# Idle row tiles of score waves filled with zero matmuls, and the last four output projections accumulated early, in a two-branch attention kernel

## The chip, the cores and the metric

The kernel runs on one core of one Trainium2 chip. The metric is the device time of the whole program in microseconds (us). Engines: PE multiplies matrices (TensorE), ACT is the scalar engine, DVE the vector engine, POOL is GpSimd, SP issues most DMAs. "Throttled window" means a stretch in which the profile shows PE's granted clock at 0.5; they are counted in units of 3.41 us, the length of a single one in the traces (three in a row: 10.24 us in that of the kernel before).

## The reference, cut to what matters

```python
S, D, H, Dh = 2048, 512, 32, 16
# branch A: softmax attention          # branch B: linear attention
scores = einsum("bhqd,bhkd->bhqk", q, k) * Dh**-0.5
a = (softmax(scores) @ v) @ wo_A
b = (phi(q) (phi(k)^T v) / (phi(q) . sum phi(k))) @ wo_B
out = g * a + (1 - g) * b              # g = sigmoid(x . gate_w), one number per row
```

Branch A needs 32 heads x 2048 x 2048 = 134 million exponentials, which fixes the shape of the kernel.

## The kernel before

The kernel is laid out at build time by a scheduler of its own, written into the kernel file. It keeps an estimated clock for each engine and at every step emits the candidate that fits best.

The work is cut into 32 rounds. A round is four heads (those of one parity among eight) for 512 queries: four row tiles of PE (32 rows each) hold the four heads. A *score unit* is one matmul with 32 rows of K as weights and 512 queries moving; units run side by side in one wave if they use different row tiles (a wave of four took 0.40 us in the trace of the kernel before, at 93.66 us, and the mean record of one matmul is 0.387). ACT takes the units in groups of three and two banks; DVE takes blocks of four units and computes the exponential with integer operations.

```python
gsets = [(0, 1, 2), (3, 4)]            # banks of ACT's groups: 3 units, 2 units, 3, 2, ...

def emit_act_group(c):
    ...
    for k, (r, kb, j) in enumerate(units):          # j: row tile of the unit
        l, q, _ = kq_aps(r, kb, j)
        fns.append(mm(BK[set_[k]], l, q))
    ride = d_ride(set(u[2] for u in units)) if n >= 2 else None   # DVE's units may ride in the same wave
    ...
    pe(fns, reads=rd, writes=wr2, waves=1, m="row", cols=128 * len(fns))
    op(AC, lambda: nc.scalar.activation(PT[...], ps[...], ACT.Exp, scale=SCALE), ...)

def warm_mm(gap):                      # "warm waves": fill PE's idle time, meant to keep its clock up
    if apos[0] >= NR or warm_count() >= WARMC:      # columns x tiles of the last 3.413 us
        return False
    ...                                # four column tiles, 17 columns of zeros each, into the accumulator
```

A wave with three units, or with two and no rider, leaves one or two row tiles idle. The accumulator `acc` is one bank into which the products of probabilities and V go, one round after the other.

Output projections: an output block of 128 rows is the sum of eight matmuls, four with branch B's numbers (transposed by DMA into `OBT`) and four with branch A's (`OT`); the last of these needs the end of the last round.

```python
def t_num(qc, q):                      # branch B: numerator, then four DMA transposes of the block
    ...
    for i in range(4):
        raw = dma(OBT[:, s, i, ...], OB[:, sl, ...], f"obt{sl}", reads=[r_OB[sl]],
                  writes=[r_OBT[s][q]] + (r_phiK[0:8] if i == 0 else []), transpose=True, lat=2.5 + i)

def t_out(qc, q):                      # eight matmuls into one bank, a copy, a DMA out
    ...
    if qc == NQC - 1 and q % 2:        # the last four: odd ones copied by ACT, even ones by DVE
        op(AC, lambda: nc.scalar.copy(outt[:, sl, :], BK[b]), reads=[r_bk[b]],
           writes=[r_outt[sl], r_wA[2], r_wv1], cost=0.48)
    ...

# main loop
if apos[0] >= NR - 1 and dst["cur"] is None and progress() > TAILP:
    maxhold[0] = 2                     # how many banks such tasks may hold at once
if apos[0] >= NR:                      # all exponentials emitted
    maxhold[0] = 6
    MISCB[:] = [6, 5] + list(range(5))
```

At the start, DVE sets to 1.0 the seventeenth column of each head of V (which gives the sums of the softmax): 512 elements of each of 128 partitions, 34 bytes apart.

The profile names a buffer by the memory that it shares: `OBT` appears there as sb_phiK, and `OB` and the rows of the output as sb_wA.

The softmax here doesn't subtract the row's maximum and nothing guards it: scores larger than these inputs give would overflow.

Of the kernel before, what the change touches and what calls it, by code (L numbers as in the profile page):

```python
# [18 lines left out]
SEMLAT = 0.05  # L19
# [126 lines left out]
def bass_gated_mix__mha_block__linear_attn_block__prompt_kernel(  # L146
# [12 lines left out]
    Dh = D // H  # L159
# [5 lines left out]
    NR = NQC * 8  # L165
# [7 lines left out]
    with ExitStack() as es:  # L173
# [164 lines left out]
        def mcost(m, waves):  # L338
            return (0.0 if m == mode[0] else 0.095) + 0.015 + 0.2145 * waves

        def pe(fns, reads=(), writes=(), waves=1.0, m="full", cols=None):
            deps = _deps_for(PE, reads, writes)
            n = len(fns)
            first = None
            cost = mcost(m, waves)
            mode[0] = m
            for k, fn in enumerate(fns):
                ev = PE.add(fn, deps if k == 0 else (), inc=(k == n - 1), cost=cost / n, lag=0.155)
                if k == 0:
                    first = ev  # L350
            first.t = ev.t
            c = 512.0 * waves if cols is None else cols
            hist.append((PE.clock, c))
            COLS.append((PE.clock, c))
            hsum[0] += c
            for res in reads:
                res.r[PE] = first
            for res in writes:
                res.w = ev
                res.r = {}  # L360
            return ev

        def mm(o, l, r, start=True, stop=True, sg=False):
# [11 lines left out]
        def load_xT(t, cc, lat):  # L375
# [29 lines left out]
        op(PO, lambda: nc.gpsimd.affine_select(out=identb[:], in_=identb[:], compare_op=ALU.not_equal,  # L405
                                               fill=1.0, base=0, pattern=[[-1, 128]], channel_multiplier=1),
           reads=[r_ident], writes=[r_ident])
        op(PO, lambda: nc.gpsimd.memset(ones[:], 1.0), writes=[r_const])
        op(PO, lambda: nc.gpsimd.memset(Zsel[:], 0.0), writes=[r_Zsel])
        op(PO, lambda: nc.gpsimd.tensor_copy(pidx[:], pidx_i[:]), reads=[r_pidx], writes=[r_mask])  # L410
# [218 lines left out]
        def t_num(qc, q):  # L629
            s = qc % 2  # L630
            sl = q % 4
            b = yield "bank"
            rd = r_phiQT[s] + [r_KVbd]
            yield ("pe", rd, [r_bk[b]], 1.4)
            pe([mm(BK[b][:, 128 * i:128 * (i + 1)], phiQT[:, s, i, 128 * q:128 * (q + 1)], KVbd[:, i, :]) for i in range(4)],
               reads=rd, writes=[r_bk[b]], waves=1.4, cols=512)
            yield ("dve", [r_bk[b], r_denB], [r_OB[sl]])
            op(DV, lambda: nc.vector.tensor_tensor(OB[:, sl, :].rearrange("p (h d) -> p h d", h=32), BK[b].rearrange("p (h d) -> p h d", h=32),
                                                   denB[:, q, :].unsqueeze(2).to_broadcast([128, 32, 16]), ALU.mult),
               reads=[r_bk[b], r_denB], writes=[r_OB[sl], r_wA[1]], cost=0.69)  # L640
            yield "free"
            for i in range(4):
                raw = dma(OBT[:, s, i, 128 * q:128 * (q + 1)], OB[:, sl, 128 * i:128 * (i + 1)], f"obt{sl}",
                          reads=[r_OB[sl]], writes=[r_OBT[s][q]] + (r_phiK[0:8] if i == 0 else []), transpose=True, lat=2.5 + i)

        def t_out(qc, q):
            s = qc % 2
# [37 lines left out]
        MPRI = 1.5  # L685
        DHUNG = -1
        DFAR = 0.8
        TAILP = 31.5
        D0 = .8
        DR0 = 1  # L690
        WARMC = 6000
# [56 lines left out]
        def need(key):  # L748
            t = bykey.get(key)
            if t is not None and not t.done:  # L750
                STATS.setdefault("forced", []).append((key, round(PE.clock, 1)))
                finish(t)

        def progress():
            return cur_units[0] / 64.0

        def misc_candidates():
            now = PE.clock
            p = progress()
            n = 0  # L760
            for t in list(tasks):
                if not t.started:
                    if t.nb > p or any(not bykey[k].done for k in t.pre):
                        continue
                if t.req == "bank":
                    free = [b for b in MISCB if b not in held]
                    if not free or len(held) >= maxhold[0]:
                        continue
                    yield (max(now, bank_free(min(free, key=bank_free)) + SEMLAT), "bank", t, 1.0)
                    n += 1  # L770
                    if n >= 3:
                        break
                    continue
                if t.done:
                    continue
                if t.req[0] == "wait":
                    if bykey[t.req[1]].done:
                        yield (now, "wait", t, 0.0)
                    continue
                if t.req[0] == "dve":  # L780
                    rt = _ready(DV, t.req[1], t.req[2]) + SEMLAT
                    if rt <= max(DV.clock, now) + 0.02:
                        yield (now, "dve", t, 0.0)
                    else:
                        yield (rt - 0.02, "dve", t, 0.0)
                else:
                    yield (_ready(PE, t.req[1], t.req[2]) + SEMLAT, "pe", t, t.req[3])
                n += 1
                if n >= 3:
                    break  # L790


# [46 lines left out]
        def act_group_cand():  # L839
# [16 lines left out]
            ready = max(_ready(PE, rd, wr), pt_free - 0.3) + SEMLAT  # L856
            return ready, units, set_, rd, wr, slot

        def emit_act_group(c):
            ready, units, set_, rd, wr, slot = c  # L860
            n = len(units)
            fns = []
            for k, (r, kb, j) in enumerate(units):
                l, q, _ = kq_aps(r, kb, j)
                fns.append(mm(BK[set_[k]], l, q))
            ride = d_ride(set(u[2] for u in units)) if n >= 2 else None
            rd, wr2 = list(rd), list(wr)
            if ride is not None:
                banks, js, rrd = ride
                fns += d_mms(banks, js)  # L870
                rd += [x for x in rrd if x not in rd]
                wr2 += [r_bk[b] for b in banks]
            pe(fns, reads=rd, writes=wr2, waves=1, m="row", cols=128 * len(fns))
            op(AC, lambda: nc.scalar.activation(PT[:, slot, 0:512 * n], ps[:, 512 * set_[0]:512 * (set_[0] + n)], ACT.Exp,  # L874
                                                scale=SCALE),
               reads=wr, writes=[r_PT[slot]], cost=EXC[n])
            if ride is not None:
                d_s1(banks, js)
            last = units[-1]
            for r in range(units[0][0], last[0]):  # L880
                act_done[r] = True
            for k, (r, kb, j) in enumerate(units):
                front[r] = max(front[r], kb + 1)
                pv_left[r] += 1
                pvq.append((r, kb, j, slot, k))
            ptleft[slot] = n
            apos[0], apos[1] = last[0], 4 * last[1] + last[2] + 1
            cur_units[0] = 64 * last[0] + 4 * last[1] + last[2] + 1
            while apos[0] < NR and apos[1] >= 4 * (NTB - claimed[apos[0]]):
                act_done[apos[0]] = True  # L890
                apos[0], apos[1] = apos[0] + 1, 0
            gcount[0] += 1
# [94 lines left out]
        dst = {"cur": None, "n": 0}  # L987
        chainq = collections.deque()
        lastd = [False]
        RES = .2  # L990
        CHG = .2
        CHI = 0.1
# [130 lines left out]

        def emit_d(c):
            _, banks, js, rd = c
            pe(d_mms(banks, js), reads=rd, writes=[r_bk[b] for b in banks], waves=1, m="row", cols=128 * len(js))
            d_s1(banks, js)

        def chain_op(_=None):
# [108 lines left out]
        need(("K", 0, 0))  # L1238
        need(("Q", 0, 0))
        op(DV, lambda: nc.vector.memset(QP[:, 1:3], 0.0), writes=r_QP[1] + r_QP[2], cost=0.9)  # L1240
        op(DV, lambda: nc.vector.memset(V[:].rearrange("p t h c -> p (t h) c")[:, :, Dh:Dh + 1], 1.0), writes=[x for v in r_V for x in v], cost=0.6)
        guard = 0
        while True:
            guard += 1
# [1 line left out]
            now = PE.clock  # L1246
            if progress() > MH2:
                maxhold[0] = 1
            if apos[0] >= NR - 1 and dst["cur"] is None and progress() > TAILP:
                maxhold[0] = 2  # L1250
            if apos[0] >= NR:
                maxhold[0] = 6
                MISCB[:] = [6, 5] + list(range(5))
            ca = act_group_cand()
# [26 lines left out]
            if not cands:  # L1281
                if not tasks and apos[0] >= NR and not pvq and not dpv:
                    break
                if apos[0] >= NR:
                    for t in tasks:
                        t.nb = -1
                    continue
                raise AssertionError(("stuck", apos, acc_round, len(pvq), [t.key for t in tasks][:5]))
            pmode = {0: "row", 0.7: "row", MPRI: "full", 1: "row", 2: "col", 3: "col", 4: "full"}
            avail = sorted((c for c in cands if c[0] <= now + 0.02),  # L1290
                           key=lambda c: (c[1] > 0 and c[2] > 0, c[1] if c[1] <= 0.7 else 1 if pmode[c[1]] == mode[0] else 2, c[1]))
            pick = None
            for c in avail:
                if c[1] == 0 or c[2] == 0.0 or now + c[2] <= must:
# [75 lines left out]
```

## Time and profile before

| | before |
|---|---|
| time, median of 3 runs | 792.84 us (791.65 to 794.0) |
| span in the profile | 790.4 us |
| ACT / PE / DVE busy | 96% / 94% / 89% |
| first exponential | 9.76 us |
| last exponential ends | 778.4 us |
| throttled windows of 3.41 us | 6 |

The page of the kernel before, its head: span, busy us and share of each engine, then the granted clock of PE in 40 equal slices (9 is 0.9 or more).

```profile
span 790.4 us, 17903 instructions
PE 743.7 (94%) x7815; PEld 227.3 (29%) x7877; DVE 701.7 (89%) x1009; ACT 760.6 (96%) x692; POOL 7.6 (1%) x35
...
PEclk9999889999999999999999999999999999999999
...
ACT 73%; PE 16%; DVE 7%; issue 3%; DMA 1%; SPq 0%
```

The last line is the chain of waits that ended last: it runs 73% through ACT. PE and DVE are nearly as full, but much of PE's time is warm waves that nobody waits for. So the first question of any change here is what it does to ACT: its work, and the time in which it waits.

The table of stages of the kernel before: stretch, its length, then busy us and count for PE, PE's weight loads, DVE, ACT and POOL, then the granted clock, the DMA share and GB/s.

```profile
0.00:20.00 20.00, 15.07 (x126) 6.83 (x127) 8.45 (x18) 10.27 (x10) 6.43 (x31) 1.00 0.80 187
80.00:100.00 20.00, 17.02 (x178) 6.70 (x174) 16.84 (x42) 17.24 (x16) 0.00 (x0) 0.86 0.00 1
100.00:120.00 20.00, 19.52 (x155) 4.94 (x157) 16.92 (x26) 17.59 (x17) 0.00 (x0) 0.89 0.03 7
420.00:440.00 20.00, 18.54 (x215) 5.17 (x208) 17.18 (x23) 18.70 (x18) 0.00 (x0) 0.91 0.18 57
440.00:460.00 20.00, 18.45 (x193) 5.16 (x195) 18.80 (x29) 19.09 (x19) 0.00 (x0) 0.91 0.01 2
760.00:780.00 20.00, 19.52 (x232) 5.62 (x230) 17.96 (x22) 17.67 (x17) 0.00 (x0) 0.92 0.01 2
```

ACT is busy for 20.00 of 20 us in most stretches. The largest exceptions are shown: the start, and stretches in which the clock is below 1. There ACT waits for scores while PE runs at half clock for a part of the stretch. In the last stretch only 0.63 us are such a wait; the rest of the missing 2.3 us is the end, since the last exponential is done at 778.4.

Three places of the trace of the kernel before, in order of time: start, length, engine, line, operation, output and inputs, count, and in brackets the idle time before and what ended it. First the ones of V on DVE, and the second wait of ACT at the start:

```profile
12.70 0.48 DVE L1241 MEMSET sb_V<- 128x512 bf16 x1 [1.70 <-issue]
14.52 1.02 ACT L874 ACTIVATE sb_PT<-ps 128x1024 bf16<-128x1024 f32 x1 [1.05 <-PE ps L364]
```

Then the gate: sixteen small copies on DVE, then the eviction that frees a bank, then the scores that waited for the bank, then ACT. The clock falls to 0.5 just after this, for three windows (94.23 to 104.47 us).

```profile
89.55 3.24 DVE L534 COPY sb_gT<-sb_g 32x16 f32<-32x16 f32 x16
92.82 0.69 DVE L1115 TENSOR_SCALAR sb_Lb<-ps 128x512 uint16<-128x512 f32 x1
93.66 0.40 PE L364 MATMUL ps<-sb_QP,sb_KT 32*128 32x512 bf16 x4 [1.89 <-DVE sb_Lb L1115]
94.10 2.36 ACT L874 ACTIVATE sb_PT<-ps 128x1536 bf16<-128x1536 f32 x2 [1.64 <-PE ps L364]
```

Last the end: the final transpose of branch A's output, then 25 matmuls (the list shows the first and the last group), and the last copy.

```profile
781.21 0.71 DVE L983 STREAM_TRANSPOSE sb_OT<-sb_Tn 128x512 bf16<-128x512 bf16 x1
781.98 0.39 PE L364 MATMUL ps<-sb_phiK,sb_OT 128*128 128x512 bf16 x1 [1.30 <-DVE sb_OT L983]
...
786.52 1.03 PE L364 MATMUL ps<-sb_phiK,sb_OT 128*128 128x512 bf16 x4
787.59 0.59 ACT L664 CAST sb_wA<-ps 128x512 bf16<-128x512 f32 x1 [2.87 <-PE ps L364]
```

### The profile page before, as it was taken

The numbers are of one execution on the slowest core, as the hardware profiler recorded it, in microseconds if no ns is written. First come the engines' busy times: TensorE is split into PE (matmuls) and PEld (weight loads), VectorE is DVE, ScalarE is ACT, GpSimd is POOL, SyncE is SP. The second block draws the span as 40 slices with busy tenths as digits, with TensorE's granted clock in tenths as the row PEclk, the third lists the DMA queues.
The fourth block names the chain that finished last, engine by engine and source line by source line (L and its number), as shares of the span: only waits on it lengthen the run. The fifth ranks groups of instructions, "written<-read, shape, count | busy, mean of one in ns | idle before, by whom it ended". The sixth has DMA issues, their size and how long they took to land.

```text
span 790.4 us, 17903 instructions
## 1 busy us (share of the span) xinstructions
PE 743.7 (94%) x7815; PEld 227.3 (29%) x7877; DVE 701.7 (89%) x1009; ACT 760.6 (96%) x692; POOL 7.6 (1%) x35
## 2 busy tenths in 40 slices
PE   7999899999999999999999999999999999999997
PEld 3333322222222222332222223223222332232222
DVE  4398889899999999989998999988999898899995
ACT  5999889999999999999999999999999999999994
POOL 3000000000000000000000000000000000000000
PEclk9999889999999999999999999999999999999999
DMA  7200000000000000102002000010001001000000
GB/s 185 70 7 2 1 7 2 7 2 9 2 5 4 2 7 2 36 1 61 2 2 61 1 8 9 16 33 8 14 17 31 10 13 24 27 10 17 12 2 27
DMA packets 31342, 14.93 MB, mean 19 GB/s; under 512 B 19104, under 2 KB 31264, under 8 KB 31264
## 3 DMA queue, kind: packets, MB, share of 16 engines
q1 hardware_dynamic: 29392, 13.00, 6.3%
q8 instruction: 62, 1.02, 0.5%
q10 hardware_dynamic: 1872, 0.79, 0.4%
q14 instruction: 16, 0.13, 0.1%
HBM read 6.55 MB, written 2.10 MB: 11 GB/s over the span
## 4 chain that ended last, share of the span: by engine, by line
ACT 73%; PE 16%; DVE 7%; issue 3%; DMA 1%; SPq 0%
ACT sb_PT L874 71%; PE ps L364 16%; DVE sb_Lb L1115 2%; ACT sb_ebuf L542 2%; DVE sb_Xb L1142 1%; DVE sb_Xb L1136 1%; DMA sb_xT<-in_A_x_dram 1%; DVE sb_Eb L1139 0%; DVE sb_Lb L1145 0%; DVE sb_gT L534 0%; DVE sb_Tn L979 0%; DVE sb_OT L983 0%; DVE sb_U L964 0%; DVE sb_QP L482 0%; DVE sb_phiK L546 0%
## 5 line engine op out<-in xcount | busy, mean ns | idle before, releaser
L874 ACT ACTIVATE sb_PT<-ps 128x1536 bf16<-128x1536 f32 (+1 forms) x655 | 752.3, 1420 | 16.6 <-PE ps L364 16.0
L364 PE MATMUL ps<-sb_QP,sb_KT 32*128 32x512 bf16 x2048 | 312.1, 387 | 25.9 <-ACT sb_PT L874 13.3
L1115 DVE TENSOR_SCALAR sb_Lb<-ps 128x512 uint16<-128x512 f32 (+1 forms) x302 | 264.8, 878 | 47.8 <-PE ps L364 46.0
L364 PEld LDWEIGHTS ps<-sb_QP,sb_KT 32*128 32x128 bf16 x2048 | 77.5, 91 | 283.8 <-ACT sb_PT L874 213.8
L364 PE MATMUL ps<-sb_PT,sb_V 128*17 128x512 bf16 x1636 | 155.7, 388 | 1.8 <-DVE sb_U L964 1.4
L364 PE MATMUL ps<-sb_warm 128*17 128x512 bf16 (+8 forms) x2074 | 147.0, 341 | 1.6 <-POOL sb_warm L402 1.3
L1142 DVE TENSOR_TENSOR sb_Xb<-sb_Xb,sb_Lb 128x2048 bf16<-128x2048 bf16 x103 | 125.1, 1214 | 0.0
L1136 DVE TENSOR_SCALAR sb_Xb<-sb_Lb 128x2048 uint16<-128x2048 uint16 x103 | 70.7, 686 | 1.4
L1139 DVE TENSOR_SCALAR sb_Eb<-sb_Lb 128x2048 uint16<-128x2048 uint16 x103 | 70.3, 683 | 0.0
L1145 DVE TENSOR_SCALAR sb_Lb<-sb_Lb 128x2048 uint16<-128x2048 uint16 x103 | 70.2, 682 | 0.0
L364 PEld LDWEIGHTS ps<-sb_PT,sb_V 128*17 128x17 bf16 x1636 | 37.2, 87 | 99.0 <-issue 89.4
L364 PEld LDWEIGHTS ps<-sb_warm 128*17 128x17 bf16 (+1 forms) x2077 | 48.2, 91 | 51.6 <-issue 27.0
L364 PE MATMUL ps<-sb_Eb,sb_V 128*17 128x512 bf16 x412 | 40.9, 388 | 0.2 <-DVE sb_Eb L1139 0.2
L364 PE MATMUL ps<-sb_Xb,sb_V 128*17 128x512 bf16 x412 | 40.4, 383 | 0.3 <-DVE sb_Xb L1142 0.2
L364 PE MATMUL ps<-sb_Lb,sb_V 128*17 128x512 bf16 x412 | 40.4, 382 | 0.1
L364 PE MATMUL ps<-sb_xT,sb_wA 128*128 128x512 bf16 x89 | 28.2, 395 | 3.1 <-issue 2.4
L964 DVE STREAM_TRANSPOSE sb_U<-ps 128x512 f32<-128x512 f32 x32 | 22.6, 708 | 3.6 <-PE ps L364 3.6
L542 ACT ACTIVATE sb_ebuf<-ps 128x512 bf16<-128x512 f32 x32 | 25.3, 791 | 0.0
L364 PE MATMUL ps<-sb_wA,sb_xT 128*128 128x128 bf16 (+1 forms) x128 | 19.0, 275 | 0.2
L364 PE MATMUL ps<-sb_xT,sb_wBx 128*128 128x512 bf16 x56 | 17.4, 383 | 1.5 <-issue 1.0
L364 PE MATMUL ps<-sb_phiK,sb_OT 128*128 128x512 bf16 x62 | 17.5, 382 | 1.3 <-DVE sb_OT L983 1.3
L466 DVE CAST sb_KT<-ps 128x512 bf16<-128x512 f32 x16 | 11.0, 685 | 8.0 <-PE ps L364 8.0
(80 smaller groups left out, 300.1 us busy)
## 6 DMA issues: line engine op xcount, KB each, us to landing
sb_QP<-sb_QT SPq DMA_DIRECT2D x120, 16.0 KB, 1.8
out_dram<-sb_wA SPq DMA_DIRECT2D x14, 128.0 KB, 1.8
sb_wA<-in_A_wqkv_dram SPq DMA_DIRECT2D x2, 512.0 KB, 6.5
sb_wBx<-in_B_wqkv_dram SPq DMA_DIRECT2D x2, 512.0 KB, 6.2
sb_xnat<-in_A_x_dram SPq DMA_DIRECT2D x2, 512.0 KB, 4.0
sb_phiK<-sb_wA SPq DMA_TRANSPOSE x64, 2.3
sb_xnat<-in_A_x_dram SPq DMA_DIRECT2D x3, 256.0 KB, 3.2
sb_wBv<-in_B_wqkv_dram SPq DMA_DIRECT2D x1, 512.0 KB, 8.5
```

Source lines behind the costliest of these rows:

```text
L364: return lambda: nc.tensor.matmul(o, lhsT=l, rhs=r, start=start, stop=stop, skip_group_check=sg)
L466: op(DV, lambda: nc.vector.tensor_copy(KT[:, t8, 512 * t:512 * (t + 1)], BK[b]), reads=[r_bk[b]], writes=[r_KT[t8][t]], cost=0.69)
L542: op(AC, lambda: nc.scalar.activation(ebuf[:, s, :], BK[b], ACT.Exp), reads=[r_bk[b]], writes=[r_e[s]], cost=0.48)
L874: op(AC, lambda: nc.scalar.activation(PT[:, slot, 0:512 * n], ps[:, 512 * set_[0]:512 * (set_[0] + n)], ACT.Exp, scale=SCALE), reads=wr, w ...
L964: op(DV, lambda: nc.vector.transpose(U[:, par, :], acc), reads=[r_acc], writes=[r_U[par]], cost=0.71)
L1115: op(DV, lambda: nc.vector.tensor_scalar(Lb[:, sl, 512 * k:512 * (k + n)], src, S1A, S1B, op0=ALU.mult, op1=ALU.add), reads=[r_bk[b] for b ...
L1136: op(DV, lambda: nc.vector.tensor_scalar(X, L, 0x7F, 0x3F00, op0=ALU.bitwise_and, op1=ALU.bitwise_or), reads=[rl], writes=[rx], cost=CH[0])
L1139: ev = op(DV, lambda: nc.vector.tensor_scalar(E_, L, 0xFF80, None, op0=ALU.bitwise_and), reads=[rl], writes=[re_], cost=CH[1])
L1142: ev = op(DV, lambda: nc.vector.tensor_tensor(xb, xb, lb, ALU.mult), reads=[rx, rl], writes=[rx], cost=CH[2])
L1145: ev = op(DV, lambda: nc.vector.tensor_scalar(L, L, float(EXP_SH), None, op0=ALU.add), reads=[rl], writes=[rl], cost=CH[3])
```

## The change

Its intent is threefold. A wave with an idle row tile gets one more matmul, a *filler*: 32 rows x 128 columns of zeros as weights, 512 columns moving, added to the accumulator, so that PE's clock falls less often. All four last output projections hold a bank each and do what they can before the last round ends. And two smaller things: the ones of V are set by POOL, and the four transposes of a block no longer wait for one another.

```diff
+        def fill(fns, rd, wr, used):
+            free = [j for j in range(4) if j not in used]
+            lj, lev = lastf
+            if lj in free:
+                free = [lj]
+            elif lev is not None and lev.t + 0.3 > PE.clock:
+                free = []
+            if FILL and free and apos[0] < NR and warm_count() < FILLC and _ready(PE, (), [r_acc]) + SEMLAT <= PE.clock:
+                j = free[0]
+                ...                    # another row tile than last time: wait for the last filler
+                fns.append(mm(acc, warm[32 * j:32 * j + 32, 0:128], warm[32 * j:32 * j + 32, :], start=False, stop=False, sg=True))
+                rd.append(r_warm)
+                wr.append(r_acc)
@@ emit_act_group, and the same in emit_d
+            fill(fns, rd, wr2, [u[2] for u in units] + (ride[1] if ride is not None else []))
+        FILL = 1
+        FILLC = 5200
@@ start
+        op(PO, lambda: nc.gpsimd.memset(V[...][:, :, Dh:Dh + 1], 1.0), ...)
-        op(DV, lambda: nc.vector.memset(V[...][:, :, Dh:Dh + 1], 1.0), ...)
@@ t_num
-                          reads=[r_OB[sl]], writes=[r_OBT[s][q]] + (r_phiK[0:8] if i == 0 else []), ...)
+                          reads=[r_OB[sl]], writes=[r_OBT[s][q]] + r_phiK[0:8] if i == 0 else [], ...)
+            r_OBT[s][q].w = _Raw(...)  # the block is there when the last of the four is
@@ main loop
-            if apos[0] >= NR - 1 and dst["cur"] is None and progress() > TAILP:
+            if apos[0] == NR - 1 and dst["cur"] is None and d_claim() is None:
+                lastp[0] = 32.0        # lets the last four projections start
                 maxhold[0] = 2
             if apos[0] >= NR:
+                lastp[0] = 32.0
                 maxhold[0] = 6
@@ choice among what is ready, once all exponentials are out: full-array work comes last
-   ... 1 if pmode[c[1]] == mode[0] else 2 ...
+   ... 5 if ended and pmode[c[1]] == "full" else 1 if pmode[c[1]] == mode[0] else 2 ...
```

(Cut: four instead of three tasks are looked at after the end, and bookkeeping of the waits.)

More of the change, by code (lines that the diff above doesn't have):

```diff
@@ L339, in mcost @@
             return (0.0 if m == mode[0] else 0.095) + 0.015 + 0.2145 * waves
+        fdeps = []
+        filler = [False]
         def pe(fns, reads=(), writes=(), waves=1.0, m="full", cols=None):
-            deps = _deps_for(PE, reads, writes)
+            deps = _deps_for(PE, reads, writes) + fdeps
+            fdeps.clear()
             n = len(fns)
@@ L360, in pe @@
                 res.r = {}
+            if filler[0]:
+                filler[0] = False
+                lastf[1] = ev
             return ev
@@ L407, in bass_gated_mix__mha_block__linear_attn_block__prompt_kernel @@
            reads=[r_ident], writes=[r_ident])
+        op(PO, lambda: nc.gpsimd.memset(V[:].rearrange("p t h c -> p (t h) c")[:, :, Dh:Dh + 1], 1.0), writes=[x for v in r_V for x in v], cost=0.6)
         op(PO, lambda: nc.gpsimd.memset(ones[:], 1.0), writes=[r_const])
@@ L643, in t_num @@
                 raw = dma(OBT[:, s, i, 128 * q:128 * (q + 1)], OB[:, sl, 128 * i:128 * (i + 1)], f"obt{sl}",
-                          reads=[r_OB[sl]], writes=[r_OBT[s][q]] + (r_phiK[0:8] if i == 0 else []), transpose=True, lat=2.5 + i)
+                          reads=[r_OB[sl]], writes=[r_OBT[s][q]] + r_phiK[0:8] if i == 0 else [], transpose=True, lat=2.5 + i)
+            r_OBT[s][q].w = _Raw(dma_sems[f"obt{sl}"][0], dma_sems[f"obt{sl}"][1], raw.t)
+            r_OBT[s][q].r = {}
+            for x in r_phiK[0:8]:
+                x.w = r_OBT[s][q].w
         def t_out(qc, q):
@@ L687, in bass_gated_mix__mha_block__linear_attn_block__prompt_kernel @@
         DFAR = 0.8
-        TAILP = 31.5
         D0 = .8
@@ L752, in need @@
                 finish(t)
+        lastp = [0.0]
         def progress():
-            return cur_units[0] / 64.0
+            return max(lastp[0], cur_units[0] / 64.0)
         def misc_candidates():
@@ L770, in misc_candidates @@
                     n += 1
-                    if n >= 3:
+                    if n >= (4 if apos[0] >= NR else 3):
                         break
@@ L788, in misc_candidates @@
                 n += 1
-                if n >= 3:
+                if n >= (4 if apos[0] >= NR else 3):
                     break
@@ L857, in act_group_cand @@
             return ready, units, set_, rd, wr, slot
+        lastf = [None, None]
+        def fill(fns, rd, wr, used):
[7 more added lines that the diff above has]
+                j = free[0]
+                lastf[0] = j
+                filler[0] = True
+                if j != lj and lev is not None:
+                    fdeps.append(_Raw(PE.sem, PE.cover(lev.idx), lev.t))
+                fns.append(mm(acc, warm[32 * j:32 * j + 32, 0:128], warm[32 * j:32 * j + 32, :], start=False, stop=False, sg=True))
+                rd.append(r_warm)
+                wr.append(r_acc)
         def emit_act_group(c):
@@ L1125, in emit_d @@
             _, banks, js, rd = c
-            pe(d_mms(banks, js), reads=rd, writes=[r_bk[b] for b in banks], waves=1, m="row", cols=128 * len(js))
+            fns, rd, wr = d_mms(banks, js), list(rd), [r_bk[b] for b in banks]
+            fill(fns, rd, wr, js)
+            pe(fns, reads=rd, writes=wr, waves=1, m="row", cols=128 * len(fns))
             d_s1(banks, js)
@@ L1240, in bass_gated_mix__mha_block__linear_attn_block__prompt_kernel @@
         op(DV, lambda: nc.vector.memset(QP[:, 1:3], 0.0), writes=r_QP[1] + r_QP[2], cost=0.9)
-        op(DV, lambda: nc.vector.memset(V[:].rearrange("p t h c -> p (t h) c")[:, :, Dh:Dh + 1], 1.0), writes=[x for v in r_V for x in v], cost=0.6)
         guard = 0
@@ L1288, in bass_gated_mix__mha_block__linear_attn_block__prompt_kernel @@
                 raise AssertionError(("stuck", apos, acc_round, len(pvq), [t.key for t in tasks][:5]))
+            ended = apos[0] >= NR
             pmode = {0: "row", 0.7: "row", MPRI: "full", 1: "row", 2: "col", 3: "col", 4: "full"}
             avail = sorted((c for c in cands if c[0] <= now + 0.02),
-                           key=lambda c: (c[1] > 0 and c[2] > 0, c[1] if c[1] <= 0.7 else 1 if pmode[c[1]] == mode[0] else 2, c[1]))
+                           key=lambda c: (c[1] > 0 and c[2] > 0, c[1] if c[1] <= 0.7 else 5 if ended and pmode[c[1]] == "full" else 1 if pmode[c[1]] == mode[0] else 2, c[1]))
             pick = None
```

## The prediction

> **What bounds it now.** ScalarE. The page gives ACT 96% busy, PE 94%, DVE 89% of 790.4 us. The chain of waits is 71% exponentials. The stage table in 20 us slices shows ACT at 20.00 of 20 almost everywhere, so only ACT's 29.8 us of idleness and its own work can be saved: about 9.8 before the first exponential at 9.76 us and some 1.5 soon after; 5.2 in 80 to 120; 2.2 in 420 to 460; 2.3 in 760 to 780, of which 0.63 is a wait and the rest is the end (the last exponential is done at 778.4); about 11 after that, where the output projections run.
>
> **The clock.** The granted clock is 0.5 in six windows: 94.2 to 104.5, 425.3 to 428.7, 449.2 to 452.6, 759.8 to 763.2. All lie on one grid of 3.413 us. [...] Each dip follows a thin window. Counting matmul records times rows times columns times 512, the windows before the dips have 41 to 47 million multiply-adds, the thinnest of the kernel (one, at 42.7, escaped). PE busy time separates them worse (2.72 us before a dip; 2.47 without one).
>
> **What changes (instruction order of both kernels).**
> 1. About 180 filler matmuls (32x128 weights, 512 columns) ride in score waves with an idle row tile; 21 fewer four-tile warm waves of 512. A wave of 3 and one of 4 tiles both take 0.39 us in the trace, so a filler should be nearly free and add 2.1 million multiply-adds, two or three per thin window. I expect the three late single dips to vanish: about 2.5 us. The one at 94 follows a stall of 1.9 us: sixteen small gate copies on DVE (3.24 us) hold back a bank. Their order is unchanged and fillers can't bridge it: it stays, unless the phase of the window is lucky. 121 PE waits on PE's own semaphore are new; I expect below 0.5 us.
> 2. Tail. Before, after the last transpose (OT, done 781.9) come 25 full matmuls (0.215 us apart, 5.4 us), and the last copy starts at 787.6. After, 21 are done earlier and only 4 follow; then two copies each on DVE (0.69) and ACT (0.59) at once. I expect about 4.2 us less; the earlier matmuls replace warm ones.
> 3. One more block of four score tiles goes to DVE (104 instead of 103): ACT has 1632 tiles instead of 1636, at 752/1636 = 0.46 us: 1.7 us less, all critical. DVE's evictions take the same time, because more are paired (129 pairs at 1.216, 158 singles at 0.684, against 110 and 192).
> 4. The memset of V (0.48 us) goes to POOL: 0.5 us of the 1.05 us wait of ACT at 13.5.
> 5. The four transposes of an output block no longer wait for each other: off the critical path, 0.
>
> Sum: 2.5 + 4.2 + 1.7 + 0.5 = 8.9 us from 792.84: **784.0 us**, range 780.5 to 788. Faster by over 2%: 0.03; within 2%: 0.96; slower: 0.01.
>
> **Right if:** three or four throttled windows left, near 95 us; ACT idle in 420 to 460 and around 764 gone; last exponential near 774; from it to the end about 8 us, not 12; exponentials' busy time near 750.5.
>
> **Wrong if:** activity is counted as busy time[...] (then fillers replace warm waves and dips increase, +3 us); waits on PE's semaphore or on the accumulator's transpose delay scores (ACT idle spread out); the dip at 94 also goes (3 us better); POOL's memset delays the first V copy.

## The result, and the profile after

The time fell to 783.16 us, median of four runs (782.51 to 784.77), against 792.89 us before (four runs, 791.65 to 794.0). Ratios in this text are the mean time of one kernel's fast runs over that of the other's of the same rounds, so not quite the ratio of the medians quoted; here it is 0.9881, with a 95% interval of 0.9859 to 0.9902.

The page of the kernel after:

```profile
span 781.7 us, 18175 instructions
PE 734.5 (94%) x7889; PEld 224.8 (29%) x7950; DVE 703.9 (90%) x997; ACT 758.6 (97%) x690; POOL 9.7 (1%) x36
...
PEclk9999889999999999999999999999999999999999
```

The table of stages of the kernel after, same columns:

```profile
0.00:20.00 20.00, 16.91 (x148) 7.58 (x149) 8.49 (x18) 11.83 (x12) 8.56 (x32) 1.00 0.78 187
80.00:100.00 20.00, 17.44 (x162) 6.18 (x160) 16.82 (x42) 15.87 (x16) 0.00 (x0) 0.79 0.00 1
100.00:120.00 20.00, 19.32 (x166) 5.20 (x166) 17.16 (x29) 19.45 (x20) 0.00 (x0) 0.95 0.03 8
440.00:460.00 20.00, 17.69 (x175) 4.70 (x171) 18.68 (x30) 19.40 (x20) 0.00 (x0) 0.91 0.01 2
460.00:480.00 20.00, 18.45 (x202) 5.71 (x203) 17.75 (x24) 19.10 (x19) 0.00 (x0) 0.91 0.03 8
```

The clock still falls near 95 us (three windows) and in two single windows, at 446 and 471 us; the one at 760 is gone. Five windows instead of six.

The start of the kernel after: the same ones on POOL, and the first V copy on DVE, which no longer waits.

```profile
1.97 2.27 POOL L415 MEMSET sb_V<- 128x512 bf16 x1
10.81 0.63 DVE L514 CAST sb_V<-ps 128x512 bf16<-128x512 f32 x1
```

The end of the kernel after: last transpose, four matmuls, and the copies on ACT, DVE and ACT.

```profile
775.36 0.71 DVE L1017 STREAM_TRANSPOSE sb_OT<-sb_Tn 128x512 bf16<-128x512 bf16 x1
776.13 1.04 PE L371 MATMUL ps<-sb_phiK,sb_OT 128*128 128x512 bf16 x4 [0.22 <-DVE sb_OT L1017]
776.77 0.58 ACT L676 CAST sb_wA<-ps 128x512 bf16<-128x512 f32 x1 [4.00 <-PE ps L371]
777.49 1.29 DVE L682 CAST sb_wA<-ps 128x512 bf16<-128x512 f32 x2 [1.42 <-ACT sb_wA L676]
778.89 0.58 ACT L676 CAST sb_wA<-ps 128x512 bf16<-128x512 f32 x1 [1.53 <-DVE sb_wA L682]
```

Where the 8.7 us between the two profiled spans (790.4 and 781.7) came from, read along ACT:

| | before | after | difference |
|---|---|---|---|
| ACT idle, 0 to 20 us | 9.73 | 8.17 | -1.6 |
| ACT idle, 20 us to the last exponential (sum over the stage tables, and one wait of 0.63 at 764) | 9.1 | 7.1 | -2.0 |
| last exponential to the end | 12.0 | 8.9 | -3.1 |
| ACT busy (whole span; exponentials 752.3 and 749.7) | 760.6 | 758.6 | -2.0 |

The four differences add up to 8.7.

### The profile page after: what moved, and what is told of

It is laid out like the page before. It is cut to its first block, busy times and chain, and to the rows that moved or that the text cites. A ratio compares the mean times of both kernels' runs of the same rounds, so it can differ in the third digit from the quotient of the medians.

```text
span 781.7 us, 18175 instructions
## 1 busy us (share of the span) xinstructions
PE 734.5 (94%) x7889; PEld 224.8 (29%) x7950; DVE 703.9 (90%) x997; ACT 758.6 (97%) x690; POOL 9.7 (1%) x36
## 4 chain that ended last, share of the span: by engine, by line
ACT 75%; PE 15%; DVE 6%; issue 3%; DVEq 0%; POOL 0%; ACTq 0%; POOLq 0%
ACT sb_PT L908 73%; PE ps L371 15%; DVE sb_Lb L1151 2%; ACT sb_ebuf L550 2%; DVE sb_Xb L1180 1%; DVE sb_Xb L1174 1%; DVE sb_Eb L1177 0%; DVE sb_Lb L1183 0%; DVE sb_xnat L554 0%; DVE sb_gT L542 0%; DVE sb_OT L1017 0%; DVE sb_Tn L1013 0%; DVE sb_U L998 0%; DVE sb_KT L474 0%; ACT sb_wA L676 0%
## 5 line engine op out<-in xcount | busy, mean ns | idle before, releaser
L908 ACT ACTIVATE sb_PT<-ps 128x1536 bf16<-128x1536 f32 (+1 forms) x653 | 749.7, 1401 | 13.0 <-PE ps L371 12.5
L371 PE MATMUL ps<-sb_QP,sb_KT 32*128 32x512 bf16 x2048 | 308.4, 387 | 28.3 <-ACT sb_PT L908 14.1
L371 PE MATMUL ps<-sb_warm 128*17 128x512 bf16 (+7 forms) x2139 | 200.6, 340 | 1.6 <-POOL sb_warm L409 1.3
L371 PEld LDWEIGHTS ps<-sb_warm 128*17 128x17 bf16 (+2 forms) x2142 | 61.4, 90 | 48.3 <-issue 25.5
L371 PE MATMUL ps<-sb_phiK 128*128 128x512 bf16 x55 | 16.9, 382 | 1.4 <-issue 1.3
```

What stands on the lines that cost most here:

```text
L371: return lambda: nc.tensor.matmul(o, lhsT=l, rhs=r, start=start, stop=stop, skip_group_check=sg)
L908: op(AC, lambda: nc.scalar.activation(PT[:, slot, 0:512 * n], ps[:, 512 * set_[0]:512 * (set_[0] + n)], ACT.Exp, scale=SCALE), reads=wr, w ...
```

## The experiments

The theory: four independent gains, one for each part of the change. Fillers keep the clock up, though PE is busy for no longer with them; the early projections shorten the end; ACT has four units less; the start has a wait less. The rivals: fillers do nothing, and what I ascribed to the clock is chance; the end is bound by the copies; the memset's gap is something else.

The kernel before was run again beside every group. Its runs spread over 789.9 to 797.0 us on those chips, so differences of one or two us are read from the profiles as well as from the times. All runs gave the right result.

| run | group | median us | mean us | ratio to before | mean granted clock of the runs |
|---|---|---|---|---|---|
| after_again | 1 | 783.15 | 783.22 | 0.9872 (0.9835 to 0.9910) | 0.9917 |
| no_fill | 1 | 785.65 | 785.84 | 0.9907 (0.9869 to 0.9946) | 0.9863 |
| no_tail | 1 | 786.72 | 786.70 | 0.9918 (0.9883 to 0.9954) | 0.9913 |
| mem_dve | 1 | 786.65 | 786.64 | 0.9917 (0.9882 to 0.9953) | 0.9892 |
| dma_back | 2 | 786.38 | 786.21 | 0.9924 (0.9897 to 0.9950) | 0.9902 |
| free_copies | 2 | 781.74 | 782.01 | 0.9871 (0.9839 to 0.9904) | 0.9912 |
| gate_pool | 2 | 779.57 | 779.82 | 0.9843 (0.9813 to 0.9873) | 0.9938 |
| fill_all | 2 | 781.84 | 781.59 | 0.9865 (0.9838 to 0.9893) | 0.9966 |
| nowarm_nofill | 3 | 834.87 | 834.79 | 1.0529 (1.0492 to 1.0565) | 0.8515 |
| nowarm_fill | 3 | 812.93 | 812.48 | 1.0243 (1.0185 to 1.0300) | 0.9130 |
| all_three | 3 | 783.01 | 783.57 | 0.9878 (0.9847 to 0.9910) | 0.9937 |
| all_three_queue | 4 | 782.55 | 782.20 | 0.9860 (0.9824 to 0.9895) | 0.9952 |

The kernel before had a mean of 793.52, 792.64, 793.24 and 793.21 us in groups 1 to 4, and a mean granted clock of 0.9866 in group 1.

### The changed kernel once more

> The changed kernel once more, for the same chip and rounds as the three beside it. Ratio to before 0.988, as in its first rounds; 4 to 6 throttled windows[...].

As expected in time. Its profile has three throttled windows (two near 95, one at 379 us), where the first profile had five. Within a profile the throttled windows start whole multiples of 3.413 us apart (before, at 94.23, 425.33, 449.22 and 759.83 us: 97, 7 and 91 times 3.413). From run to run their place changes: the first near 95 starts at 94.23 us before, 91.63 after, 95.34 in after_again and 94.94 in no_fill, which are no such multiples apart. Its start was slower: the first exponential came at 11.39 us instead of 9.66. The eight matmuls of the first projection took 3.57 us instead of 1.89, as at half clock, though the clock row still shows 1.00 there. The reason for that 1.00 is in the packed trace: its record of the clock begins only at 10.0 us here, and the row counts a stretch without a record as full clock. The same late start (11.5 us) is in the profiles of no_tail and all_three_queue, whose records begin at 10.0 and 10.4 us; in the other eleven profiles they begin at 4.1 to 6.4 us and the first exponential comes at 9.6 to 10.1. So the late start goes with a later first record of the clock; that PE ran at half clock until then is an estimate from the 3.57 and 1.89 us. The late start is part of the spread between runs of one kernel, and the mean granted clock doesn't show it.

### Without fillers

```diff
-        FILL = 1
+        FILL = 0
```

> The changed kernel without fillers, all else kept (21 idle-tile fillers' worth of warm waves come back by themselves: 1088 instead of 1040 warm matmuls of 512). Theory[...]: the dips near 425 to 475 and 760 come back, 6 or more throttled windows, 1.0 to 2.5 us slower than the changed kernel. Rival (activity is busy time, the fillers do nothing or displace useful warm waves): 4 or 5 windows, within 0.5 us of the changed kernel.

785.84 against 783.22 us in the same group: 2.6 us slower. Its profile shows eight windows (two near 98, three at 306 to 317, and single ones at 450, 569 and 689 us). ACT is idle for 10.2 us between 80 and 700 us, against 5.3 us in the profile of after_again: 4.9 us for five more windows, so about 1.0 us for each. Over the timed runs the granted clock averages 0.9863, as in the kernel before (0.9866), and 0.9917 with fillers. The theory holds on the average. It is not that every run gains: without fillers the six runs have clocks from 0.979 to 0.993, and the one at 0.993 took 782.4 us, as fast as the kernel with fillers at that clock (782.1 to 784.2 us). So a filler itself costs nothing that shows here.

### The old end

```diff
-            if apos[0] == NR - 1 and dst["cur"] is None and d_claim() is None:
-                lastp[0] = 32.0
+            if apos[0] >= NR - 1 and dst["cur"] is None and progress() > 31.5:
                 maxhold[0] = 2
@@ and no lastp, three tasks, no rank 5 for full-array work
```

> The changed kernel with the old end: output projections of the last rows not held back and accumulated early. From the last exponential to the end 12.0 us again in place of 8.9, so 3.1 us slower than the changed kernel. Rival (the end is bound by the copies and the DMA, not by the matmuls): below 1 us slower.

3.5 us slower in the mean. From the last exponential (773.04 us) to the end of the span (784.8 us) it takes 11.8 us, against 9.0 in after_again, with three windows in both profiles. The theory holds: the 21 matmuls moved ahead of the last transpose are what the end gains. (The edit takes back the whole change of the end, so its smaller parts are not told apart.)

### The ones of V on DVE again

```diff
-        op(PO, lambda: nc.gpsimd.memset(V[...][:, :, Dh:Dh + 1], 1.0), ...)
+        op(DV, lambda: nc.vector.memset(V[...][:, :, Dh:Dh + 1], 1.0), ...)      # after the memset of QP
```

> The changed kernel with the memset of V's ones back on DVE; the rest of the order is the same. Theory (the 1.70 us of DVE idle ahead of that memset belong to the memset itself, of which the profile shows only the last 0.48): the idle time comes back ahead of it, ACT is idle 1.4 to 1.6 us longer in the first 20 us, 1.5 us slower than the changed kernel. Rival (an instruction fetch stalls DVE at that place): the stall does not follow the memset, difference 0.5 us or less.

The idle time came back with the memset. From the trace of mem_dve:

```profile
12.71 0.48 DVE L1278 MEMSET sb_V<- 128x512 bf16 x1 [1.70 <-issue]
13.77 0.40 PE L458 MATMUL ps<-sb_identb,sb_xnat 128*128 128x128 bf16 x4 [2.09 <-DVE sb_V L513]
16.89 1.45 ACT L907 ACTIVATE sb_PT<-ps 128x1536 bf16<-128x1536 f32 x1 [1.34 <-PE ps L371]
```

On POOL the same memset is recorded with 2.27 us, and 1.70 + 0.48 = 2.18. So I estimate from these that the whole instruction takes about 2.2 us on either engine, and that on DVE the record shows only its last 0.48. The gap went with the memset (1.70 us ahead of it in before and in mem_dve, no gap at that place of DVE in after), so the rival, by which it stays in its place, is out. ACT is idle for 10.75 us in the first 20, against 8.17 in the first profile after, 2.6 more: PE's wait of 2.09 us in that trace was followed by a throttled window of its own (15 to 18 us), which the profile of the kernel before did not have. The mean is 3.4 us slower, more than I expected; which part of that beyond the 2.6 us is the spread of the runs is left open.

### The transposes wait for each other again

```diff
-   writes=[r_OBT[s][q]] + r_phiK[0:8] if i == 0 else [], ...
+   writes=[r_OBT[s][q]] + (r_phiK[0:8] if i == 0 else []), ...
@@ and without the lines that set the block's time to that of its last transpose
```

> The changed kernel with the four transposes of an output block waiting for each other again. The build shows what the prediction missed: with that wait the scheduler gives DVE 103 blocks instead of 104 and pairs fewer evictions (107 pairs, 198 singles). Theory (the shorter wait is what moves the block of four tiles from ACT to DVE): exponentials busy 1.8 us longer, 1.5 to 2.0 us slower than the changed kernel (ratio about 0.990). Rival (off the critical path, 0, as predicted): within 0.5 us of the changed kernel.

786.21 us, 3.0 us above the mean of after_again, which ran in another group; set against the kernel before of its own group it is 3.9 us (6.4 us below it, after_again 10.3). That is more than expected either way. Its profile can be set beside the first profile after, with the same five windows in the same places:

| | after | dma_back |
|---|---|---|
| span | 781.7 | 784.7 |
| exponentials busy | 749.7 | 751.7 |
| last exponential to end | 8.9 | 10.05 |

2.0 + 1.1 = 3.1 us, which is the whole difference of the spans (3.0). No engine waits longer for a transpose; what changes is what the scheduler makes of it: 103 blocks on DVE instead of 104, a last group of a single unit on ACT, and 107 paired evictions (one DVE instruction that reads two score banks) instead of 129. The second term is new: the last DVE block is ready later against ACT's last exponential, so the accumulator's transpose follows that exponential by 1.6 us (776.23 - 774.65) instead of 0.5 (773.27 - 772.77). The rival "0, off the critical path" was my own prediction, and it is wrong.

### The last copies without turns

```diff
 odd (ACT):
-   reads=[r_bk[b]], writes=[r_outt[sl], r_wA[2], r_wv1], ...
+   reads=[r_bk[b]], writes=[r_outt[sl]], ...
 even (DVE):
-   reads=[r_bk[b]], writes=[r_outt[sl], r_wA[2], r_wv1], ...
+   reads=[r_bk[b]], writes=[r_outt[sl]] + ([r_wA[2], r_wv1] if qc < NQC - 1 else []), ...
```

> The changed kernel, but the last four output copies no longer all write the two resources that stand for the long finished value weights, so that DVE and ACT needn't take turns. Theory (the turns cost the 1.1 us by which the end fell short of the predicted 4.2): last exponential to end 7.9 us instead of 8.9 to 9.0, 1.0 us faster than the changed kernel. Rival (the copies are bound by the four last matmuls or the output DMA): the end stays at 8.9.

The instruction order is the same; only waits are gone. The end of its trace, to be set beside that of the kernel after:

```profile
774.60 0.71 DVE L1017 STREAM_TRANSPOSE sb_OT<-sb_Tn 128x512 bf16<-128x512 bf16 x1
775.36 1.04 PE L371 MATMUL ps<-sb_phiK,sb_OT 128*128 128x512 bf16 x4 [0.22 <-DVE sb_OT L1017]
775.79 1.29 DVE L682 CAST sb_wA<-ps 128x512 bf16<-128x512 f32 x2 [0.48 <-PE ps L371]
776.01 0.58 ACT L676 CAST sb_wA<-ps 128x512 bf16<-128x512 f32 x1 [4.00 <-PE ps L371]
777.09 0.58 ACT L676 CAST sb_wA<-ps 128x512 bf16<-128x512 f32 x1 [0.49 <-ACT sb_wA L676]
```

DVE and ACT now copy at the same time. From the end of the last transpose to the start of the last copy it is 1.8 us (777.09 - 775.31) instead of 2.8 (778.89 - 776.07), and from the last exponential to the end 7.9 us instead of 8.9. The times do not show it: 782.01 us is 1.2 us below after_again, but only 0.3 us if each is set against the kernel before of its own group.

### The gate copies on POOL

```diff
-   op(DV, lambda j=j, a=a: nc.vector.tensor_copy(gv[32 * j:32 * j + 32, :, a], g0[32 * a:32 * a + 32, :]), ..., cost=0.08)
+   op(PO, lambda j=j, a=a: nc.gpsimd.tensor_copy(gv[32 * j:32 * j + 32, :, a], g0[32 * a:32 * a + 32, :]), ..., cost=0.25)
```

> The changed kernel with the sixteen small gate copies on POOL instead of DVE. Theory (their 3.24 us on DVE hold back a bank, PE idles 1.9 us, and the two or three throttled windows after it follow from that): the dip near 95 is gone, ACT idle in 80 to 120 below 1.5 us instead of 4.3 to 4.7, 3 us faster than the changed kernel, granted clock 0.995 or more. Rival (the windows near 95 come from the projections there, not from the gate copies): the dip stays, at most 1.6 us faster.

779.82 us, the fastest kernel. After_again ran in another group: the means differ by 3.4 us, and by 2.5 us if each is set against the kernel before of its own group (12.8 and 10.3 us below it). The intervals of the two ratios overlap, so the profile has to carry the rest. From its trace: the copies on POOL, the eviction on DVE right beside them, and what waits for the copies.

```profile
87.74 4.72 POOL L542 COPY sb_gT<-sb_g 32x16 f32<-32x16 f32 x16 [68.97 <-DVE sb_g L537]
88.33 0.69 DVE L1151 TENSOR_SCALAR sb_Lb<-ps 128x512 uint16<-128x512 f32 x1 [0.45 <-PE ps L371]
92.56 0.19 DVE L1011 TENSOR_TENSOR sb_rden<-sb_rden,sb_gT 128x32 f32<-128x32 f32 x1 [2.55 <-POOL sb_gT L542]
94.88 0.39 PE L371 MATMUL ps<-sb_PT,sb_V 128*17 128x512 bf16 x4 [1.46 <-DVE sb_U L998]
```

PE no longer stops while the copies run. But DVE waits 2.55 us for them (POOL needs 4.72 us for what DVE did in 3.24), the transpose of the accumulator stands behind it in DVE's order, and PE then waits 1.46 us for that transpose (the last line). So the stall became shorter and came later. ACT is idle for 1.9 us in 80 to 120, against 4.7 in the first profile after. One throttled window is left there (96 to 100 us, right after the new stall), against two or three. I had expected that none would be left, and below 1.5 us; but the theory, that most of these windows follow from the gate copies, holds. The mean granted clock also missed the 0.995 that I expected: 0.994 to 0.997 in four of the five runs, and 0.990 in the profiled one, the slowest (782.21 us), which has three more throttled windows elsewhere (305, 376 and 731 us).

### Fillers without limit

```diff
-        FILLC = 5200
+        FILLC = 8192
```

> The changed kernel with the limit on fillers lifted (activity bound 8192 instead of 5200): 606 matmuls of that form instead of 195, 17 fewer warm waves of 512. Theory (a filler is activity and costs nothing): only the windows after the gate stall near 95 remain, clock 0.993 or more in every run, 0 to 1 us faster than the changed kernel. Rival (fillers and their waits on PE's own semaphore cost time): slower by 0.5 us or more at the same clock.

The granted clock is 0.995 to 0.998 in every run, the highest of the kernels with the old gate. The profile has two throttled windows, one near 95 as expected, and one at 237 us, which was not. The time is 781.59 us, 1.6 us below after_again of the other group, or 0.8 us if each is set against the kernel before of its own group. 0.0049 more clock is by estimate 2 x 0.0049 x 781 / 3.413 = 2.2 windows fewer (each has half the clock for 3.413 us), about 2 us at the 1.0 us each of no_fill. So a part of what the clock promises arrives. The waits on PE's own semaphore are in its list with 4.6 us in 29 waits (0.6 us in 4 in the kernel after); the rival's slowdown does not appear, but a cost of up to about 1 us is not excluded by these times. This is one limit of the change: with its bound of 5200, most idle row tiles stay idle.

### Without warm waves, with and without fillers

```diff
-        WARMC = 6000
+        WARMC = 0
@@ nowarm_nofill: FILL = 0; nowarm_fill: FILLC = 8192
```

> The changed kernel with neither warm waves nor fillers after the start (so that only useful matmuls are left). Both theories: many more throttled windows; granted clock below 0.95, slower than the kernel before by 5 us or more. It is the base for the next run.

> The same without warm waves, but with 583 fillers in score waves that run anyway (no limit). PE's busy time stays within 5 us of the run without them, since a filler runs beside its wave. Theory[...]: the granted clock rises clearly, at least half of the throttled windows of the base go, and time falls by 5 us or more. Rival (activity is busy time): same clock within 0.005, same time within 2 us.

The span, the busy time and the clock rows of the pages, first without fillers:

```profile
span 831.9 us, 13774 instructions
PE 732.6 (88%) x5758; PEld 195.0 (23%) x5816; DVE 707.7 (85%) x996; ACT 769.3 (92%) x690; POOL 10.1 (1%) x36
...
PEclk9999798958578686799897989799989989976758
```

and with fillers:

```profile
span 806.6 us, 15319 instructions
PE 695.6 (86%) x6339; PEld 197.1 (24%) x6399; DVE 705.6 (87%) x996; ACT 764.0 (95%) x690; POOL 10.1 (1%) x36
...
PEclk9999897999989687899899987999989999996999
```

The theory was that fillers, which add nothing to PE's busy time, take throttled windows away all the same. Without either, 73 windows are throttled and the time is 834.8 us: the warm waves are worth some 49 us (no_fill, which has them and no fillers, took 785.8 us in another group). 583 fillers, which all run beside scores that run anyway, take 36 of the 73 windows away in the profile, and 22 us in the mean; the clock of the timed runs rises from 0.8515 to 0.9130. I had expected PE's busy time to stay within 5 us; it fell (732.6 to 695.6 us, at a clock of 0.92 instead of 0.85 in the profiles). So the fair comparison is in the windows at full clock alone: there PE was busy for 2.94 of 3.41 us without fillers and for 2.91 with them. So PE's busy time alone does not account for the 36 windows.

Busy time fails in the kernel before too: a window in which PE was busy for 2.72 of its 3.41 us (756.4 to 759.8 us) was followed by a throttled one, and five others at full clock, with 2.47 to 2.70 us, were not. Whether the clock goes by how much of the array is in use, by the number of matmuls or by something else, no run separates; it was not shown.

### All three improvements together

This is the kernel after with the gate copies on POOL, the last copies without turns, and fillers without limit.

> The changed kernel with the gate copies on POOL, the last copies freed of their turns, and no limit on fillers. If the three effects add (3.4, 1.1 and 1.0 to 1.5 us) 777.5 to 778.5 us, ratio to before about 0.981, clock 0.997 or more, at most two throttled windows, last exponential to end 7.9 us.

It missed: 783.57 us in the mean, 780.7 to 787.9. In the profile, which is of the fastest of the six runs, the windows are gone but for one (clock 0.997) and the end is short (8.2 us), but there is a new wait. (The other runs have clocks from 0.988 to 0.998, so in some of them windows remain.) The list of waits of all_three, who waited for what, us in total, times, longest:

```profile
PE ps L371 <- DMA sb_phiK<-sb_wA: 2.7, 1, 2.7
ACT sb_PT L908 <- PE ps L371: 2.6, 1, 2.6
```

The second line is the same list for 555 to 585 us only. At 564 us PE waits 2.7 us for a transposed block of branch B, and ACT stands still for 2.6 us. No profile of before, after, groups 1 and 2 or the pair without warm waves has a wait of PE for such a transpose. Three changes at once had moved the projection too close behind its transposes. That wait explains 2.6 us of the profiled run, not the whole distance of the mean from 778.

### The same, with a queue for the transposes in the scheduler

```diff
             for i in range(4):
+                obtq[0] = max(SP.clock, obtq[0]) + 1.5
-                ... transpose=True, lat=2.5 + i)
+                ... transpose=True, lat=obtq[0] - SP.clock + 1.5)
```

> The run of all three with one thing more: the kernel's own scheduler is told that transposes of output blocks go through the DMA queue one after the other, 1.5 us each (nine of them took 13.99 us in the trace of the run of all three), instead of 2.5 to 5.5 us from the issue whatever is queued. Theory (that run missed its 778 because an output projection was put too early and PE waited 2.7 us for a transpose, with ACT idle 2.6 us): no wait of PE for such a transpose, 777.5 to 779 us, ratio to before 0.980 to 0.983. Rival (three changes at once cost something else, for example unlimited fillers): still 782 us or more.

The rival's number: 782.20 us, and the wait is still there. From its list of waits, and its trace of SP's queue:

```profile
PE ps L371 <- DMA sb_phiK<-sb_wA: 2.0, 1, 2.0
...
554.94 4.94 SPq L308 DMA_DIRECT2D sb_QP<-sb_QT  x8
559.97 12.16 SPq L304 DMA_TRANSPOSE sb_phiK<-sb_wA  x8
```

My model of the queue was incomplete: eight copies of Q stood in it ahead of the transposes for 4.94 us, so the first transpose began at 559.97, though the block was there at 557.2 (the DVE operation that makes it began at 556.56 and took 0.68). Whether the three gains add to 778 us once that wait is gone has not been tried. What makes some runs of all_three slower still (787.9 us at a clock of 0.988) is open too.

## Why the prediction was right

The total was right: 784.0 predicted, 783.16 measured, inside the range. The mechanisms were largely right; three of the five terms were mis-sized, in ways that cancelled. That the sum came out within 1 us is in part luck.

| term of the sum | predicted | profile before and after | by undoing it |
|---|---|---|---|
| 1 fillers, fewer throttled windows | 2.5 | 2.0 | 2.6 |
| 2 the end | 4.2 | 3.1 | 3.5 |
| 3 one block from ACT to DVE | 1.7 | 2.0 | 3.0, together with 5 |
| 4 ones of V on POOL | 0.5 | 1.6 | 3.4 |
| 5 transposes without waits | 0 | (in 3) | (in 3) |

The last column adds up to 12.5 us, more than the 10.3 us between after_again and before in group 1 (793.52 - 783.22). Undoing a part reorders the schedule behind it, and each mean has the spread of six runs; it is a check of each part, not a sum.

**Fillers: right in effect and in average size; wrong in which windows.** I expected the three late single windows to vanish, and three or four in all to be left. Five were left in the first profile: of the late ones two vanished (425 and 760 us), one stayed near its place (446 us) and a new one came at 471; on the average over runs the clock rose by 0.005. My count of multiply-adds separated thin windows in the trace of before (with matmuls across a border shared between windows, the windows at full clock ahead of a throttled one have 28.9 to 36.7 million, all others at full clock 37.5 or more, from 16 to 770 us). In that of after it did so less well: counted in the same way, those ahead of 446 and 471 have 36.2 and 39.3 million, and two others, with 36.3 and 38.9, were not punished. So multiply-adds are not the whole of it either, and the right measure was not found. Records of matmuls can be missing from a trace, so the count is not exact. The rival, activity as busy time, is refuted by the pair without warm waves. "It stays", of the dip at the gate, was right, and gate_pool shows why.

**The end: the mechanism was right, the size too large by 1.1 us.** The failing step is "then two copies each on DVE (0.69) and ACT (0.59) at once". They did not run at once: all four copies write the resources `r_wA[2]` and `r_wv1`, so each engine waited for the other, 1.4 and 1.5 us in the waits' list. free_copies gets 1.0 us of it back.

**The block: right, 1.7 predicted and 2.0 measured (ACT's busy time; 2.6 in the line of the exponentials alone); but its cause was misplaced.** The step that failed is "The four transposes of an output block no longer wait for each other: off the critical path, 0." On the chip the wait was indeed off the path. In the scheduler it was not: dma_back shows that these lines alone are what gives DVE the 104th block and the pairs.

**The ones of V: 0.5 predicted, 1.6 measured.** I costed the memset by its record, 0.48 us. The 1.70 us of idle time in front of it were by my estimate part of it; in mem_dve they came back with it. (Both profiles have the early start; in that of after_again the late start hides the gain, with ACT idle for 9.9 us in the first 20.)

**Waits on PE's own semaphore: below 0.5 us predicted;** the list of waits of after has 0.6 us of them in 4 waits, that of before none. What they cost the whole was not measured apart.

## What to carry to other kernels

If a scheduler decides the order, cost a change by what it does to the order and not only by its waits on the chip: a wait that nobody on the critical path felt moved 2 us of work to another engine. Read idle time just before an instruction as possibly part of it, above all where it reads "issue" and has no releaser (here 1.70 us ahead of a record of 0.48). And ask of a clock that falls now and then what stood still in the window before: here moving sixteen copies of 0.2 us each to an idle engine brought 2.5 to 3.4 us (with intervals that overlap), about as much as the fillers that the change brought.
